# A 12-unit attention and rational-activation kernel: a new table of steps, and one PSUM slot for each chunk of the last unit

## Chip, cores and metric

The kernel runs on one core of a Trainium2 chip. The metric is device time in microseconds of one execution; 226.9 us is the median of three runs of the kernel before (226.29 to 226.97). The profile is of one further execution.

## What is computed

The reference, cut to what matters:

```python
# q, k, v, f_logit: (B, H, S, D) = (4, 8, 768, 48)
f = 1.0 / (1.0 + np.exp(-f_logit))
for t in range(S):
    state = f[:, :, t, :, None] * state + einsum('bhd,bhe->bhde', k[:, :, t], v[:, :, t])
    y[:, :, t] = einsum('bhd,bhde->bhe', q[:, :, t], state)
x = y.transpose(0, 2, 1, 3).reshape(3072, 384)
h = x @ w_in                                   # w_in (384, 2048)
P = a[0] + a[1] * h + a[2] * h**2 + a[3] * h**3
Q = 1.0 + abs(b[0]) * abs(h) + abs(b[1]) * h**2
out = (P / (Q + 1e-6)) @ w_out                 # w_out (2048, 384), out (3072, 384) f32
```

A gated linear attention with a recurrent state is followed by a two-layer feed-forward with a rational activation.

## The kernel before

The 4 batches times 768 tokens are cut into 12 units of 256 tokens (two chunks of 128). Unit n belongs to batch n mod 4; the state of a batch is handed from unit n to unit n + 4. Every unit passes through the same list of steps, each a small function of the kernel, and the program is one table, `ORDER`, of such steps. A step appends its instructions to its engines' queues in the order of the table, and semaphores between the engines follow from the data. The engines run their own queues in order, so the table sets two things: the order of steps on each engine, and which PSUM slot (`@0` to `@3`, two banks each, one tile at a time) a step takes. A step that takes a slot waits until the last reader of the slot's tile before it is done.

The steps by engine, with the unit as first argument and a range of blocks of 128 columns of d_ff (0 to 16) or of head pairs (0 to 4) as the last ones:

- SP's queue: `ld n f`, `ld n k`, `ld n q` (loads, L200), `ab_` (two small loads of coefficients for all partitions, L228 and L230), `so`, `s0` (stores, L584; `s1` issues on ACT's queue).
- POOL: `ld n v` (a load that casts to bf16), `wi` and `wo` (weights, L216 and L220), `vm` (copies of v, L388; `vm 0` on ACT), `zd` (L525) and `ta` (L559), which are DMAs that accumulate: z += h2 and gall += hy. `ca` and `cb` make the triangular and the identity matrix.
- ACT: `ef`, `ls` (log of the gate, L308, L313), `A` (exponentials of its running sum, L332), `ye` (L456), `ae` (L461), `hy` (PSUM to SBUF, L488), `sa` (square, L496), `ln` and `lz` (log of Q, L516 and L532), `ex` (1/Q by exp, L540), `oe` (result from PSUM to `osb`, L590).
- DVE: `xa` (scaled q and k, L337), `Te` (L356), `mk` (masked scores `scm`, L377), `st` (state, L465), `sq` (L492), `ab` (absolute value, L500), `p1`, `p2`, `pm`, `tv` (the polynomial, L545, L550, L555, L563), `gm` (times 1/Q, L568), `cz`, `cc`, `fa`, `fb` (constants), and `hv 0` (L210), a memset on `w_in_sb` behind which the `wi` loads wait.
- PE: `cs` (running sum, L323), `T` (transposes, L348), `sc` (scores, L369), `sv`, `id` (state, L413, L424, L428), `yb` (attention output, L394), `h` (x times w_in, L474), `u` (sums h2 and |h| in PSUM, L508), `o` (times w_out, L575; 12 units, two chunks j, 16 blocks m).

For half of the units' blocks Q is summed by PE (`u`, then `ln`), for the others by a DMA (`zd`, then `lz`); `ta` adds the two parts of the polynomial by a DMA, `tv` does it on DVE in the first unit and for half of the last. `hy` has three buffers, `h2` and `z` two, `gall` three, f, k, q and v three each, `osb` two.

In the last unit both chunks of the result lie in one tile, `op`, of slot 2. Chunk 1 is copied by DVE (`oe 11 1 2 v`), chunk 0 by ACT (`oe 11 0 1 s`):

```python
if sl is not None:
    s["op"] = slot(sl, [P, UB, 512], F32, "op")
for m in range(m0, m1):
    nc.tensor.matmul(s["op"][:, j, 0:DM], s["g"][:, m, C * j:C * j + C], w_out_sb[:, m, :],
                     start=(m == 0), stop=(m == KF - 1))
```

Of the kernel before, what the change touches and what calls it, by code (L numbers as in the profile page):

```python
# [19 lines left out]
b1_; cz 3; cb; ld 0 f 2 4; ld 0 f 0 2; ca; cz 0; ld 0 q 2 4; cz 2; ld 0 k 2 4; cz 1; cc; ef 0 2 4  # L20
ld 0 k 0 2; fa 0; ls 0 2 4; ld 0 q 0 2; ef 0 0 2; cs 0 2 4 @0; ls 0 0 2; ld 0 v; A 0 0 2 4
id 0 0 @1; A 0 1 2 4; xa 0 0 2 4; rg; cs 0 0 2 @2; ld 1 f; xa 0 1 2 4; ae 0; A 0 1 0 2; hv 0; ab_
T 0 2 4 @0; wi 0 4; A 0 0 0 2; xa 0 1 0 2; Te 0 2 4; xa 0 0 0 2; sc 0 1 @0; ld 1 k; T 0 0 2 @2
wi 4 8; mk 0 1; vc 0; Te 0 0 2; vm 0 0 s; sv 0; vm 0 1 s; ld 1 v; sc 0 0 @2; st 0 0; ld 1 q; wi 8 16
mk 0 0; id 0 1; st 0 1; yb 0 0 4 @2; ef 1; ld 2 f; fa 1; ls 1; ye 0; cs 1 @1; fb; h 0 0 4 @2; A 1 0
A 1 1; h 0 4 8 @1; hy 0 0 4; xa 1 1; ld 2 k; id 1 0 @2; hy 0 4 8; xa 1 0; ld 2 q; ae 1; sv 1; vm 1 0
vm 1 1; ab 0 0 8; T 1 @1; ld 2 v; sq 0 0 8; Te 1; u 0 0 4 @0; ef 2; ld 3 f; u 0 4 8 @3; st 1 0
# [603 lines left out]
```

## Time and profile before

| | |
|---|---|
| median of three runs | 226.9 us |
| profiled execution: its own time | 224.9 us |
| profiled execution: span of the program | 223.2 us |
| busy PE, DVE, ACT, POOL | 205.2, 203.3, 201.1, 70.4 us |
| TensorE clock granted | 1.00 of full speed |
| HBM read and written | 25.2 and 4.7 MB |

The profiled execution was 2.0 us shorter than the median of the runs. Its time is the span and 1.7 us around it. A row of the page gives line, engine, operation, tiles, shape and count, then busy time and mean duration, then idle time of the engine just before and what ended it. A line of the timeline gives start, length, engine, line, operation, and in brackets the idle time before it and the releaser.

### The profile page before, as it was taken

Reading aid. Unit: us, or ns where it says so; the run is one execution under the profiler, and the core shown is the slowest. Engines: PE = TensorE matmul, PEld = TensorE weight load, DVE = VectorE, ACT = ScalarE, POOL = GpSimd, SP = SyncE. Lnnn points to the kernel's source line nnn. Section 1 sums busy time; section 2 is a strip of 40 time slices with the busy share of each in tenths; the row PEclk is TensorE's granted clock in tenths of the full one; section 3 lists DMA queues with packets and bytes.
Section 4 is the critical chain, followed back from the end, with each engine's and each line's share of the span. In section 5 each row is a group of like instructions: output and inputs, shape, how many; then the busy total and the mean of one; then the engine's idle time right before and its main releaser. Section 6 shows DMA issues by size and latency. Waiting matters only on the chain.

```text
span 223.2 us, 7133 instructions
## 1 busy us (share of the span) xinstructions
PE 205.2 (92%) x3128; PEld 144.0 (65%) x3128; DVE 203.3 (91%) x248; ACT 201.1 (90%) x215; POOL 70.4 (32%) x94
## 2 busy tenths in 40 slices
PE   1786799999999997999999999999999999999991
PEld 1544378566766686567777668678578587785550
DVE  6865999999789997999999999999999999999960
ACT  5645599999999999999999999999999999999960
POOL 3662930021500333107334244041395311341000
PEclk9999999999999999999999999999999999999998
DMA  6999999998999999977999999938869999597434
GB/s 156 225 230 210 237 202 204 193 248 232 170 180 244 243 184 216 260 193 144 171 233 248 209 238 244 213 74 134 171 117 184 207 188 212 112 206 150 94 91 120
DMA packets 61984, 42.33 MB, mean 190 GB/s; under 512 B 51458, under 2 KB 57346, under 8 KB 61954
## 3 DMA queue, kind: packets, MB, share of 16 engines
q0 software_dynamic: 19648, 22.61, 61.6%
q1 hardware_dynamic: 42144, 19.08, 35.0%
q8 instruction: 24, 0.39, 0.6%
q10 hardware_dynamic: 162, 0.20, 0.2%
q14 instruction: 6, 0.05, 0.1%
HBM read 25.17 MB, written 4.72 MB: 134 GB/s over the span
## 4 chain that ended last, share of the span: by engine, by line
PE 62%; ACT 20%; DMA 7%; SPq 4%; issue 3%; DVE 3%
PE op L575 26%; PE hp L474 18%; DMA fn<-in_f_logit_dram 7%; PE u L508 5%; ACT hy L488 4%; PE y L394 4%; ACT lq L516 4%; ACT qi L540 3%; PE tp L348 3%; SPq L200 3%; ACT h L496 3%; ACT A L332 3%; PE sc L369 2%; ACT lsp L313 1%; ACT fn L308 1%
## 5 line engine op out<-in xcount | busy, mean ns | idle before, releaser
L474 PE MATMUL hp<-xT,w_in_sb 128*128 128x256 bf16 x576 | 68.6, 274 | 2.3 <-issue 1.3
L575 PE MATMUL op<-w_out_sb,gall 128*128 128x384 bf16 x384 | 68.7, 326 | 1.1 <-DVE osb L590 0.6
L474 PEld LDWEIGHTS <-w_in_sb 128*128 128x128 bf16 x576 | 55.9, 98 | 12.8 <-issue 3.6
L488 ACT CAST hy<-hp 128x1024 bf16<-128x1024 f32 x48 | 49.5, 1050 | 4.1 <-PE hp L474 4.0
L575 PEld LDWEIGHTS <-gall 128*128 128x128 bf16 x384 | 36.3, 98 | 25.0 <-issue 1.8
L540 ACT ACTIVATE qi<-lq 128x2048 bf16<-128x2048 f32 (+1 forms) x25 | 46.4, 1874 | 0.0
L559 POOL DMA_DIRECT2D gall<-hy x21 | 21.3, 1109 | 64.1 <-PE hp L474 16.4
L377 DVE TENSOR_TENSOR scm<-sc,mask 128x1024 bf16<-128x1024 f32 x24 | 28.7, 1217 | 3.3 <-PE sc L369 3.3
L568 DVE TENSOR_TENSOR gall<-gall,qi 128x2048 bf16<-128x2048 bf16 (+1 forms) x25 | 29.5, 1181 | 0.7 <-ACT qi L540 0.6
L555 DVE TENSOR_TENSOR gall<-gall,h 128x2048 bf16<-128x2048 bf16 (+1 forms) x25 | 29.3, 1177 | 0.0
L388 POOL COPY vmp<-vn 128x128 bf16<-128x128 bf16 x22 | 18.1, 927 | 22.9 <-DMA vn<-in_v_dram 22.9
L525 POOL DMA_DIRECT2D z<-h x12 | 13.2, 1097 | 37.9 <-ACT xT L456 13.4
L516 ACT ACTIVATE lq<-u 128x1024 f32<-128x1024 f32 x24 | 24.5, 1048 | 0.3 <-PE u L508 0.3
L532 ACT ACTIVATE lq<-z 128x2048 f32<-128x2048 bf16 x12 | 23.5, 1956 | 0.0
L492 DVE TENSOR_TENSOR h<-hy 128x2048 bf16<-128x2048 bf16 (+1 forms) x18 | 20.9, 1166 | 0.5 <-ACT hy L488 0.5
L332 ACT ACTIVATE A<-cs 128x768 f32<-128x768 f32 (+1 forms) x26 | 18.9, 786 | 0.7 <-PE cs L323 0.5
L500 DVE TENSOR_SCALAR z<-hy 128x2048 uint16<-128x2048 uint16 (+1 forms) x25 | 16.8, 676 | 1.5 <-ACT hy L488 1.5
L550 DVE TENSOR_SCALAR hy<-hy,a_sb 128x4096 bf16<-128x4096 bf16 (+2 forms) x15 | 16.9, 1128 | 0.1
L545 DVE TENSOR_SCALAR gall<-hy,a_sb 128x4096 bf16<-128x4096 bf16 (+2 forms) x15 | 16.9, 1126 | 0.0
L323 PE MATMUL cs<-lsp,Ui 128*128 128x384 bf16 (+1 forms) x39 | 11.1, 345 | 4.8 <-ACT lsp L313 4.6
L308 ACT ACTIVATE fn<-fn 128x768 f32<-128x768 f32 (+1 forms) x13 | 10.8, 830 | 4.8 <-DMA fn<-in_f_logit_dram 4.8
L356 DVE COPY qkT<-tp 128x2048 bf16<-128x2048 bf16 (+1 forms) x13 | 14.8, 1135 | 0.4 <-PE tp L348 0.4
(69 smaller groups left out, 272.9 us busy)
## 6 DMA issues: line engine op xcount, KB each, us to landing
gall<-hy POOLq DMA_DIRECT2D x21, 512.0 KB, 7.8
z<-h POOLq DMA_DIRECT2D x12, 512.0 KB, 7.3
fn<-in_f_logit_dram SPq DMA_DIRECT2D x11, 384.0 KB, 13.2
kn<-in_k_dram SPq DMA_DIRECT2D x11, 384.0 KB, 11.9
qn<-in_q_dram SPq DMA_DIRECT2D x11, 384.0 KB, 10.6
out_dram<-osb SPq DMA_DIRECT2D x22, 192.0 KB, 4.2
vn<-in_v_dram POOLq DMA_DIRECT2D x11, 192.0 KB, 8.8
w_out_sb<-in_moe_w_out_dram POOLq DMA_DIRECT2D x4, 384.0 KB, 11.6
```

Source lines behind the costliest of these rows:

```text
L332: nc.scalar.activation(t, src, AF.Exp, scale=1.0 if x else -1.0)
L377: nc.vector.tensor_mul(t, s["sc", g].rearrange("s r a i t -> s (r a) (i t)"), mb)
L474: nc.tensor.matmul(t[:, m - m0, :].rearrange("f (j t) -> f j t", j=UB), w_in_sb[:, kk, m * P:(m + 1) * P], s["x"][:, :, kk, :], start=(kk ...
L488: nc.scalar.copy(fl(big(s, "hy", "hy", 3), m0, m1), fl(s["hp", m0], 0, m1 - m0))
L492: nc.vector.tensor_mul(fl(big(s, "h2", "h2", 2), m0, m1), fl(s["hy"], m0, m1), fl(s["hy"], m0, m1))
L516: nc.scalar.activation(fl(s["lq", g], m0 - 8 * g, m1 - 8 * g), fl(s["u", m0], 0, m1 - m0), AF.Ln, scale=rsig2, bias=1.0 + 1e-6)
L532: nc.scalar.activation(fl(s["lq", g], m0 - 8 * g, m1 - 8 * g), fl(s["z"], m0, m1), AF.Ln, scale=rsig2, bias=1.0 + 1e-6)
L540: nc.scalar.activation(fl(s["qi", g], m0 - 8 * g, m1 - 8 * g), fl(s["lq", g], m0 - 8 * g, m1 - 8 * g), AF.Exp, scale=-1.0)
L555: nc.vector.tensor_mul(fl(s["g"], m0, m1), fl(s["g"], m0, m1), fl(s["h2"], m0, m1))
L559: nc.gpsimd.dma_start(out=fl(s["g"], m0, m1), in_=fl(s["hy"], m0, m1), accum_op=ALU.add)
L568: nc.vector.tensor_mul(fl(s["g"], m0, m1), fl(s["g"], m0, m1), fl(s["qi", g], m0 - 8 * g, m1 - 8 * g))
L575: nc.tensor.matmul(s["op"][:, j, 0:DM], s["g"][:, m, C * j:C * j + C], w_out_sb[:, m, :], start=(m == 0), stop=(m == KF - 1))
```

## The change

The table `ORDER` holds the same steps in another order, on every engine, and partly in other slots. Two steps go and four come: the copies of the last unit's chunks, `oe 11 1 2 v` and `oe 11 0 1 s`, are each replaced by two copies of half the columns, `oc 11 j 0 s` on ACT and `oc 11 j 1 v` on DVE. For the last unit `o` takes a slot for each chunk (`@1` and `@3`) in place of one for both. `wm`, a step that neither table calls, gets a wider tile. The steps on SP's and POOL's queues move too: `ld 1 q` ahead of `ld 1 k`, `ab_` behind both, `ld 4 f`, `ld 5 f` and `ld 6 f` further ahead among k and q, `ld 3 v` ahead of the `wo` loads, `ca` ahead of `cb`.

The beginning, some lines of the middle and the end of the table, and the code:

```diff
 ORDER = """
-b1_; cz 3; cb; ld 0 f 2 4; ld 0 f 0 2; ca; cz 0; ld 0 q 2 4; cz 2; ld 0 k 2 4; cz 1; cc; ef 0 2 4
-ld 0 k 0 2; fa 0; ls 0 2 4; ld 0 q 0 2; ef 0 0 2; cs 0 2 4 @0; ls 0 0 2; ld 0 v; A 0 0 2 4
-id 0 0 @1; A 0 1 2 4; xa 0 0 2 4; rg; cs 0 0 2 @2; ld 1 f; xa 0 1 2 4; ae 0; A 0 1 0 2; hv 0; ab_
-T 0 2 4 @0; wi 0 4; A 0 0 0 2; xa 0 1 0 2; Te 0 2 4; xa 0 0 0 2; sc 0 1 @0; ld 1 k; T 0 0 2 @2
-wi 4 8; mk 0 1; vc 0; Te 0 0 2; vm 0 0 s; sv 0; vm 0 1 s; ld 1 v; sc 0 0 @2; st 0 0; ld 1 q; wi 8 16
-mk 0 0; id 0 1; st 0 1; yb 0 0 4 @2; ef 1; ld 2 f; fa 1; ls 1; ye 0; cs 1 @1; fb; h 0 0 4 @2; A 1 0
-A 1 1; h 0 4 8 @1; hy 0 0 4; xa 1 1; ld 2 k; id 1 0 @2; hy 0 4 8; xa 1 0; ld 2 q; ae 1; sv 1; vm 1 0
-vm 1 1; ab 0 0 8; T 1 @1; ld 2 v; sq 0 0 8; Te 1; u 0 0 4 @0; ef 2; ld 3 f; u 0 4 8 @3; st 1 0
-ln 0 0 4; p1 0 0 8; id 1 1; sc 1 0 @1; ln 0 4 8; st 1 1; sc 1 1 @0; mk 1 0; ls 2; ex 0 0 8; mk 1 1
-id 2 0 @3; ld 3 k; cs 2 @1; pm 0 0 8; yb 1 0 4 @0; A 2 1; wo 8 12; h 0 12 16 @2; p2 0 0 8; ye 1
+cz 2; ca; ld 0 f 2 4; cz 0; ld 0 f 0 2; ld 0 q 2 4; cb; cc; cz 1; ld 0 k 2 4; cz 3; ld 0 k 0 2
+ef 0 2 4; ld 0 q 0 2; ls 0 2 4; ef 0 0 2; cs 0 2 4 @0; ld 0 v; b1_; ls 0 0 2; ld 1 f; A 0 0 2 4
+cs 0 0 2 @1; A 0 1 2 4; id 0 0 @2; A 0 1 0 2; hv 0; xa 0 1 2 4; wi 0 4; xa 0 0 2 4; ae 0; A 0 0 0 2
+ld 1 q; T 0 2 4 @0; ld 1 k; xa 0 0 0 2; xa 0 1 0 2; fa 0; T 0 0 2 @1; vc 0; ab_; wi 4 8; sv 0
+Te 0 2 4; rg; st 0 0; vm 0 0 s; ld 1 v; Te 0 0 2; ef 1; ld 2 f; id 0 1; sc 0 1 @0; st 0 1; wi 8 16
+sc 0 0 @1; ls 1; mk 0 0; vm 0 1 s; id 1 0 @2; cs 1 @3; mk 0 1; A 1 1; yb 0 0 4 @0; ye 0; A 1 0
+h 0 0 4 @0; fa 1; xa 1 0; ld 2 k; h 0 4 8 @3; hy 0 0 4; ld 2 q; xa 1 1; ae 1; fb; hy 0 4 8; T 1 @0
+sq 0 0 8; sv 1; vm 1 1; vm 1 0; ab 0 0 8; ef 2; ld 3 f; ld 2 v; p1 0 0 8; u 0 0 4 @3; ls 2; ld 3 v
+Te 1; u 0 4 8 @1; ln 0 0 4; wo 4 8; st 1 0; sc 1 0 @0; wo 0 4; ln 0 4 8; cs 2 @3; mk 1 0; sc 1 1 @1
+A 2 1; mk 1 1; h 0 12 16 @0; ex 0 0 8; pm 0 0 8; yb 1 0 4 @1; ld 3 k; xa 2 1; id 1 1; ye 1; p2 0 0 8
...
-o 0 1 4 8; ex 1 0 8; h 2 0 4 @2; pm 1 0 8; ld 5 f; gm 0 8 16; h 2 4 8 @0; hy 2 0 4; xa 3 1; ef 4
-o 0 1 8 12; sq 1 8 16; ld 5 k; o 0 1 12 16; sa 2 4 8; ld 4 v; sv 3; sa 2 0 4; p2 1 0 16; o 0 0 8 12
-vm 3 0; ls 4; vm 3 1; ld 5 q; u 1 12 16 @2; st 3 0; ta 1 0 8; hy 2 4 8; pm 1 8 16; o 0 0 12 16
-ln 1 12 16; id 3 1; ld 6 f; T 3 @0; st 3 1; ta 1 8 16; ef 5; ab 2 0 8; u 1 8 12 @3; Te 3; oe 0 0 2 s
-zd 2 0 8; h 2 12 16 @2; ln 1 8 12; so 0 0 2; ls 5; sc 3 1 @3; sc 3 0 @0; h 2 8 12 @1; mk 3 1; ld 6 k
-ex 1 8 16; ld 5 v; mk 3 0; cs 4 @3; vm 4 1; hy 2 8 12; vm 4 0; cs 5 @0; A 4 0; yb 3 0 4 @1; gm 1 0 8
-A 4 1; ye 3; xa 4 0; o 1 0 0 4 @3; hy 2 12 16; o 1 1 0 4; xa 4 1; ld 6 q; h 3 4 8 @1; A 5 0
+o 0 0 0 4 @2; ex 0 8 16; st 3 0; yb 2 0 4 @3; tv 0 8 16; id 3 1; ld 5 v; o 0 1 0 4; st 3 1; ye 2
+o 0 0 4 8; gm 0 8 16; vm 3 1; ln 1 4 8; h 2 4 8 @3; p1 1 0 16; ls 4; ex 1 0 8; o 0 1 4 8; xa 3 0
+h 2 0 4 @0; ld 6 f; ab 1 8 16; ld 4 q; hy 2 4 8; pm 1 0 8; o 0 1 8 12; o 0 0 8 12; sa 2 0 4
+sq 1 8 16; T 3 @1; ef 5; o 0 1 12 16; p2 1 0 16; hy 2 0 4; ld 5 k; o 0 0 12 16; sa 2 4 8
+u 1 8 12 @0; Te 3; ta 1 0 8; oe 0 0 2 s; u 1 12 16 @3; ab 2 0 8; ln 1 8 12; sc 3 0 @2; sc 3 1 @1
+ln 1 12 16; mk 3 0; h 2 8 12 @0; ls 5; mk 3 1; cs 4 @2; hy 2 8 12; ld 6 k; cs 5 @3; pm 1 8 16
+ld 5 q; A 4 0; yb 3 0 4 @0; ld 7 f; A 4 1; xa 4 0; h 2 12 16 @1; ta 1 8 16; ye 3; xa 4 1; vm 4 1
+A 5 0; vm 4 0; h 3 0 4 @0; gm 1 0 8; hy 2 12 16; vm 5 1; zd 2 0 8; A 5 1; T 4 @2; p1 2 0 16; ld 6 v
...
-st 4 1; pm 2 0 8; ld 8 f; sv 5 @2; oe 1 0 2 s; id 5 0; ef 7; sq 3 0 8; T 5 @3; ta 2 0 8; so 1 0 2
-sv 6 @3; ln 3 8 12; gm 2 0 8; id 6 0; cs 7 @1; ld 9 f; ae 6; ln 3 12 16; st 6 0; sc 5 1 @2; pm 3 0 8
+p2 2 0 16; ln 2 8 12; o 1 0 8 12; xa 5 1; hy 3 12 16; ta 2 0 8; o 1 1 8 12; ld 8 f; pm 2 8 16
+h 3 8 12 @1; A 6 0; st 5 0; so 1 0 2; zd 3 0 8; gm 2 0 8; ef 7; id 5 1; h 4 8 12 @3; ld 7 v; A 6 1
...
-ta 4 8 16; o 3 1 0 4; gm 3 8 16; ae 7; ef 9; yb 6 0 4 @0; lz 4 0 8; st 7 0; o 3 0 4 8; p1 5 0 16
-gm 4 8 16; o 3 1 12 16; sa 6 0 4; o 4 0 0 4 @3; Te 7; hy 6 0 4; o 4 1 0 4; ld 11 f; ef 10; sq 6 8 16
+pm 4 8 16; o 3 1 0 4; ae 7; ye 6; o 3 0 4 8; st 7 0; ta 4 8 16; p1 5 0 16; ex 4 0 8; o 3 1 4 8
+hy 6 8 12; gm 4 8 16; T 7 @3; A 8 0; o 4 0 0 4 @2; ab 5 8 16; hy 6 4 8; o 4 0 4 8; Te 7; sa 6 4 8
...
-ln 11 12 16; o 10 1 12 16; pm 11 8 12; o 11 0 0 4 @2; p2 11 8 12; ex 11 8 12; tv 11 8 12; o 11 1 0 4
-ex 11 12 16; o 11 0 4 8; gm 11 8 12; o 11 1 4 8; oe 10 0 2 s; gm 11 12 16; o 11 1 8 12; so 10 0 2
-o 11 1 12 16; o 11 0 8 12; oe 11 1 2 v; o 11 0 12 16; s1 11 1 2; s0 11 1 2; oe 11 0 1 s; s1 11 0 1
+o 11 0 0 4 @1; ex 11 8 12; tv 11 8 12; o 11 1 0 4 @3; tv 11 12 16; ex 11 12 16; o 11 0 4 8
+gm 11 8 12; o 11 1 4 8; oe 10 0 2 s; gm 11 12 16; o 11 1 8 12; so 10 0 2; o 11 1 12 16; o 11 0 8 12
+oc 11 1 0 s; oc 11 1 1 v; o 11 0 12 16; s1 11 1 2; s0 11 1 2; oc 11 0 0 s; oc 11 0 1 v; s1 11 0 1
 s0 11 0 1
 """
...
     def o(n, j, m0, m1, sl=None):
         s = unit(n)
-        if sl is not None:
-            s["op"] = slot(sl, [P, UB, 512], F32, "op")
+        if sl is not None and n == B * NCC - 1:
+            s["op", j] = slot(sl, [P, 512], F32, "op")
+        elif sl is not None:
+            t = slot(sl, [P, UB, 512], F32, "op")
+            s["op"] = t
+            for i in range(UB):
+                s["op", i] = t[:, i]
         for m in range(m0, m1):
-            nc.tensor.matmul(s["op"][:, j, 0:DM], s["g"][:, m, C * j:C * j + C], w_out_sb[:, m, :],
+            nc.tensor.matmul(s["op", j][:, 0:DM], s["g"][:, m, C * j:C * j + C], w_out_sb[:, m, :],
                              start=(m == 0), stop=(m == KF - 1))
...
+    def oc(n, j, c, eng):
+        s = unit(n)
+        if "osb" not in s:
+            s["osb"] = ms.tile([P, UB, DM], F32, name="osb")
+        cc = slice(c * DM // 2, (c + 1) * DM // 2)
+        (nc.scalar.copy if eng == "s" else nc.vector.tensor_copy)(s["osb"][:, j, cc], s["op", j][:, cc])
```

## The prediction

> **What bounds the kernel now.** I read the page's busy shares, then its chain, then the waits of each engine, then the timeline at the places that the waits name. The shares and the chain:
>
> ```profile
> PE 205.2 (92%) x3128; PEld 144.0 (65%) x3128; DVE 203.3 (91%) x248; ACT 201.1 (90%) x215; POOL 70.4 (32%) x94
> PE 62%; ACT 20%; DMA 7%; SPq 4%; issue 3%; DVE 3%
> ```
>
> Three engines are within 2% of each other, so none is the bound alone. The chain has three stages: loads until 24.8 us, ACT until 63.8, PE to the end. The joints show in the timeline (start, length, engine, operation, idle before it and who ended it):
>
> ```profile
> 24.80 0.84 ACT L308 ACTIVATE fn<-fn 128x768 f32<-128x768 f32 x1 [3.42 <-DMA fn<-in_f_logit_dram]
> 26.61 0.42 PE L369 MATMUL sc<-qkT 48*64 48x128 bf16 x16 [0.91 <-ACT lq L516]
> ...
> 59.38 2.36 DVE L377 TENSOR_TENSOR scm<-sc,mask 128x1024 bf16<-128x1024 f32 x2 [1.20 <-PE sc L369]
> 63.05 0.96 DVE L337 TENSOR_TENSOR qkp<-qn,A 128x768 bf16<-128x768 f32 x1 [0.17 <-ACT A L332]
> 65.37 0.69 DVE L500 TENSOR_SCALAR z<-hy 128x2048 uint16<-128x2048 uint16 x1 [0.49 <-ACT hy L488]
> ...
> 85.56 1.38 PE L474 MATMUL hp<-xT,w_in_sb 128*128 128x256 bf16 x11 [1.14 <-issue]
> ...
> 217.67 0.56 DVE L590 COPY osb<-op 128x384 f32<-128x384 f32 x1 [1.81 <-PE op L575]
> 218.28 0.81 PE L575 MATMUL op<-w_out_sb,gall 128*128 128x384 bf16 x4 [0.65 <-DVE osb L590]
> 219.13 0.48 ACT L590 COPY osb<-op 128x384 f32<-128x384 f32 x1 [3.31 <-PE op L575]
> ```
>
> Line 1 is step `ef 2`: ACT stood idle 3.4 us for unit 2's f_logit. The next four are handovers between engines in a bad order. The 1.14 us of "issue" is no step's fault. The last three are the tail: PE has its last 4 matmuls left and waits 0.65 us for a DVE copy.
>
> **PE's account.** Successive rows overlap slightly, so I count from start to start: `h` 1.31 us, four matmuls of `o` 0.65, `u` 0.86, `yb` 1.12 (0.97 for units 0 to 3), `T` 0.89, `cs` 0.66, `sc` 0.33, `sv` 0.37, `id` 0.38 or 0.16. From `cs 2` at 28.47 there stand 46 `h`, 96 quarters of `o`, 22 `u`, 11 `yb`, 10 each of `T`, `cs` and `sv`, 20 `sc`, 15 `id`: 183.6 us. PE ends at 219.09, so it loses 219.09 - 28.47 - 183.6 = 7.0 us: 0.8 in the tail (the wait and its drain), 1.3 to "issue", 4.9 waiting for ACT and DVE in many small pieces.
>
> [...] Between 29 and 38 us the two queues moved nearly equal counts of packets of very unequal size:
>
> ```profile
> q0 software_dynamic: 1638, 1.20, 85.7%
> q1 hardware_dynamic: 1615, 0.61, 38.8%
> ```
>
> [...] the 0.65 us come from both being one tile. [...]
>
> **The change, part by part.**
>
> *Tail.* With a slot for each chunk, PE no longer waits for the copy of chunk 1: -0.65 us, and nothing is late next, since `o 11 0 12 16` reads `gall` made long before. The last copy falls from 128x384 (0.48) to halves on ACT and DVE. The 128x768 copy takes 0.84, so 384 columns cost 0.36 and half a copy 0.48 - 0.18 = 0.30: -0.18. Two instructions are added (one ACT, one DVE, 0.3 each), both where those engines are idle. The two stores of each chunk now wait for both copies. The edit of `wm` issues nothing: neither table calls it. Sum -0.8; bounds -0.5 and -1.0.
>
> *Reordering, 29 to 210 us.* No other step is added or removed. What an order costs can be read without a clock: follow a loop of steps over the engines and add the work along it. Before, `h 2 0 4` (PE) feeds `hy 2 0 4` (ACT); from there to the end of `hy 2 12 16` ACT has 14.7 us of work (with `ef 4`, `ls 4`, `ef 5`, `ex 1 8 16` between); that feeds `ab 2 8 16` on DVE, which stands 6.9 us of work behind `st 3 1`; and `st 3 1` frees the slot of `u 1 8 12`, which stands 6.2 us behind `h 2 0 4` on PE. 14.7 - 6.9 - 6.2 = 1.6, with three handovers of 0.1 about 1.9 us that somebody must idle. The three DVE waits of 1.20, 0.17 and 0.49 above are just that: 1.86. In the new order the four ACT steps leave this stretch, so ACT's leg is 9.6, and `st 3 1` stands eight places earlier on DVE: the loop is slack. I took the worst such loop in each stretch of about 30 us. Before: 0.25, 1.9, 0.7, 0.8, 0.4, 0.85, together 4.9, which is what the account found. After: 1.1, 0.05, 0.25, 0.15, 0.3, 0.9, together 2.7. So -2.2 us; bounds 0 (other waits come in their place) and -3.5.
>
> *Accumulating DMAs (POOL's queue).* The new order leaves less room between a `ta` and the `gm` that reads it. For `gm 4 8 16` DVE has 6.5 us of other work after `pm 4 8 16` (16 before), for `gm 2 0 8` 6.7 (11 before), 1 0 8 6.9, 5 0 8 7.7. The page's median from issue to landing is 7.8 us and the issue lags some 0.5:
>
> ```profile
> gall<-hy POOLq DMA_DIRECT2D x21, 512.0 KB, 7.8
> ```
>
> but `ta 1 0 8` took 4.7 when its queue was empty. At 4.7 there is no wait; at 8.3 the four cost 1.8 + 1.6 + 1.4 + 0.6 = 5.4 us on DVE, and PE soon waits with it. I take +0.8; bounds 0 and +5.4.
>
> *Prologue.* `hv 0`, the memset that holds the w_in loads back, moves before the first `xa` (some 4.5 us instead of 6.97), so POOL's `wi` packets start 2 to 3 us earlier and share the DMA engines with unit 0's v (landing 9.37). `sv 0` now stands ahead of `sc 0 1` and `sc 0 0` on PE and waits for v, so `yb 0` comes 2 to 3 us later than 13.0. Cover: ACT has 3.4 us to spare before `ef 2`. `ab_` (1.9 us of SP issue) moves behind `ld 1 q` and `ld 1 k`, which refills SP's queue sooner; `ld 2 f` keeps its place there with the same packets ahead. Its landing stays near 24.8, give or take 1.5 for the altered mixing. Then `ls 2` at once, `cs 2` at 27.3 instead of 28.5, but `sc 1 1` waits for `ln 0 4 8` until 28.2 (26.6 before), so `h 1 4 8` starts near 31.7 against 31.51. Net +0.5; bounds -1 and +2.5. [...] `o 0 0 0 4` needs w_out only at 45. Later SP loads (`ld 5 f`, `ld 6 f` ahead of q and k) keep 27 us or more from a free buffer to the first use, against landings of 11 to 13: nothing, covered by ACT's and PE's own work; late SP stores wait behind loads with nobody waiting but the buffer `osb`.
>
> Sum: -0.8 - 2.2 + 0.8 + 0.5 = -1.7 on the profiled execution, 223.2 us of span to 221.5, its own time 224.9 to 223.2. The median of the runs shown is 226.9, 2.0 above that execution, so 225.2.
>
> **Rivals.**
> 1. *The new order works as above:* 225.2, from 223 to 226.2. For it: the loop at 58 to 66 us is in the trace to a tenth. Chance 0.50.
> 2. *The gain is eaten:* waits removed return as small ones, or `ld 2 f` lands 1.5 later, which delays ACT and through its slots PE, one for one. -0.8 - 2.2 + 0.8 + 2.0 is close to 0: about 226.8. Chance 0.13.
> 3. *Slower by the accumulating DMAs:* with landings at 8 us or more, `gm` waits on DVE at four to six places; `o`, `mk` and `st` queue behind it, and PE and ACT with them. -0.8 - 2.2 + 5.4 + 0.5 = +2.9: 229.8; half of that price, 227 to 228. It decides from about 2.5 us of such waits on. For it: 7.8 is a median, and the room is under it at four places; before, only `gm 1 0 8`, `gm 2 8 16` and three near the end had so little. Against it: unstacked transfers land in 4.5 to 5.1. With a late `ld 2 f` on top it gives the upper end. Chance 0.37.
> 4. *The slot change does nothing* (the copies still serialise): 0.8 us less gain, inside the cases above.
>
> **The numbers.** A measurement of this kernel can tell about 0.3% (0.7 us) from no change. Faster 0.50, within 0.13, slower 0.37. The range for 8 in 10 runs from 222.4 (the loops at -3.5, a prologue at -0.5) to 229.6 (rival 3 whole); the likeliest case's own range is 223 to 226.2.
>
> **What would show it.** Right: no PE wait for `osb`, two copies of 128x192 on each engine, DVE's waits for `scm` and ACT's for `hy` under half of what the waits between 28.5 and 216 us list before (2.8 and 2.1 us). Wrong: DVE waits of over 0.5 us at L568's counterpart ended by a DMA (rival 3); `ef 2` after 26 us (rival 2); PE waiting on ACT evenly all along would mean that ACT, not the order, sets the pace.

## The result, and the profile after

The changed kernel takes **233.7 us** (median of four runs, 232.69 to 234.65) where the kernel before took 226.6 beside it: a ratio of **1.031**, with an interval of 1.026 to 1.037. That is slower, by 7 us, and beyond the upper end of the predicted range. The profiled execution took 234.3 us, with a span of 232.6.

The page of the kernel after begins with the busy time of each engine; further down stand the shares of the chain that ended last, by engine and by line:

```profile
PE 209.2 (90%) x3113; PEld 146.0 (63%) x3128; DVE 205.4 (88%) x249; ACT 202.2 (87%) x216; POOL 71.6 (31%) x94
DVE 26%; DMA 23%; issue 15%; PE 15%; ACT 13%; SPq 4%; POOL 1%; ACTq 0%; DVEq 0%; POOLq 0%
DMA gall<-hy 12%; DMA b<-in_moe_b_dram 6%; PE op L582 5%; DMA z<-h 5%; DVE gall L556 4%; SPq L201 4%; DVE scm L378 4%; PE hp L475 4%; DVE gall L569 3%; DVE h L493 3%; DVE qkp L338 3%; ACT qi L541 3%; PE u L509 3%; DVE gall L546 2%; DVE z L501 2%
```

Busy time hardly moved; the idle time is what grew. Before, PE held 62% of the chain and DMA 7%. Now PE holds 15% and DMA 23%, and the DMAs at the head of the second list are the two kinds of accumulating transfer (`gall<-hy` is `ta`, `z<-h` is `zd`) and a load of 1 KB, `b`. So transfers now stand on the chain that ended last. Which of them cost time is a question for the experiments.

The account of the prediction (starts of PE's steps, less their work) places the loss. "Loss" is time from one start to the other minus the work of the steps between:

| | before | after | difference |
|---|---|---|---|
| start of `h 1 4 8` | 31.5 | 38.3 | +6.8 |
| loss from `h 1 4 8` to `h 5 0 4` | 4.7 | 3.4 | -1.3 |
| loss from `h 5 0 4` to `h 9 0 4` | 0.7 | 4.7 | +4.1 |
| loss from `h 9 0 4` to `o 11 0 12 16` | 1.4 | 0.6 | -0.8 |

With 0.4 us of work that has moved across the first mark this is the 9.1 us by which PE's last four matmuls start later (227.4 against 218.3); the copies behind them add 0.3. The medians differ by less, 7 us, because the profiled execution of the kernel before was 1.7 us under its median. The first row varies most between executions: the new start came to `h 1 4 8` at 37.0 in a joined kernel below, and the old start at 33.3 in the kernel with the new tail alone. In two of four stretches the change gained what was forecast in kind; the start and the third stretch lost far more.

**The start.** Lines of the timeline of DVE (start, length, engine, line, operation, and in brackets the idle time before it and who ended it):

```profile
24.28 0.17 DVE L278 TENSOR_SCALAR bm<-b 128x2 uint32<-128x2 uint32 x1 [8.68 <-DMA b<-in_moe_b_dram]
25.44 0.96 DVE L338 TENSOR_TENSOR qkp<-qn,A 128x768 bf16<-128x768 f32 x1
26.31 0.95 DVE L338 TENSOR_TENSOR qkp<-kn,A 128x768 bf16<-128x768 f32 x1
```

The first line is `fa 1`, waiting 8.7 us for `ab_`'s load, which was issued at 10.47 and took 13.8 us (4.5 before). Behind it in DVE's queue stand `xa 1 0` and `xa 1 1`. Before, they stood at 19.35 and 17.49, and `xa 1 0` waited for q:

```profile
17.49 0.96 DVE L337 TENSOR_TENSOR qkp<-kn,A 128x768 bf16<-128x768 f32 x1 [2.14 <-ACT A L332]
19.35 0.96 DVE L337 TENSOR_TENSOR qkp<-qn,A 128x768 bf16<-128x768 f32 x1 [0.90 <-DMA qn<-in_q_dram]
```

The wait for `b` looks like the whole cause of the late start. The experiments show that it isn't.

**The middle.** The waits between 40 and 229 us (engine, line, for whom: total, times, longest), then the place of the longest in the timeline:

```profile
ACT lq L533 <- DMA z<-h: 2.7, 2, 2.3
DVE gall L569 <- DMA gall<-hy: 2.3, 5, 0.9
DVE scm L378 <- PE sc L370: 0.6, 3, 0.2
ACT hy L489 <- PE hp L475: 0.4, 2, 0.2
```

```profile
119.23 1.91 ACT L533 ACTIVATE lq<-z 128x2048 f32<-128x2048 bf16 x1 [2.26 <-DMA z<-h]
121.24 0.56 DVE L466 TENSOR_TENSOR state<-sv,alast 128x384 bf16<-128x384 f32 x1 [1.78 <-ACT alast L462]
121.85 0.32 PE L425 MATMUL sv<-state,ident 128*128 128x384 bf16 x1 [1.48 <-DVE state L466]
161.94 1.23 DVE L569 TENSOR_TENSOR gall<-gall,qi 128x2048 bf16<-128x2048 bf16 x1 [0.89 <-DMA gall<-hy]
```

The last two of the waits are those of the loops, 2.8 and 2.1 us before: the new order did remove them. The first two did not exist before. The timeline shows how one wait travels: `lz 4 0 8` stands idle on ACT for `zd 4 0 8` (11.2 us from issue to landing; 7.8 before), so `ae 7` behind it is late, so `st 7 0` on DVE, so `id 7 1` on PE.

**The tail:**

```profile
226.94 0.32 ACT L605 COPY osb<-op 128x192 f32<-128x192 f32 x1 [1.14 <-PE op L582]
227.29 0.36 DVE L605 COPY osb<-op 128x192 f32<-128x192 f32 x1 [1.46 <-ACT osb L605]
228.27 0.32 ACT L605 COPY osb<-op 128x192 f32<-128x192 f32 x1 [1.01 <-PE op L582]
228.62 0.36 DVE L605 COPY osb<-op 128x192 f32<-128x192 f32 x1 [0.97 <-ACT osb L605]
```

PE waits for no copy any more. But DVE's half waits for ACT's half: the two run one after the other, 0.7 us where one copy of the whole chunk took 0.48.

### The profile page after: what moved, and what is told of

It reads as the page before. It is cut to its first block, busy times and chain, and to the rows that moved or that the text cites. A ratio compares the mean times of both kernels' runs of the same rounds, so it can differ in the third digit from the quotient of the medians.

```text
span 232.6 us, 7113 instructions
## 1 busy us (share of the span) xinstructions
PE 209.2 (90%) x3113; PEld 146.0 (63%) x3128; DVE 205.4 (88%) x249; ACT 202.2 (87%) x216; POOL 71.6 (31%) x94
## 4 chain that ended last, share of the span: by engine, by line
DVE 26%; DMA 23%; issue 15%; PE 15%; ACT 13%; SPq 4%; POOL 1%; ACTq 0%; DVEq 0%; POOLq 0%
DMA gall<-hy 12%; DMA b<-in_moe_b_dram 6%; PE op L582 5%; DMA z<-h 5%; DVE gall L556 4%; SPq L201 4%; DVE scm L378 4%; PE hp L475 4%; DVE gall L569 3%; DVE h L493 3%; DVE qkp L338 3%; ACT qi L541 3%; PE u L509 3%; DVE gall L546 2%; DVE z L501 2%
## 5 line engine op out<-in xcount | busy, mean ns | idle before, releaser
L475 PE MATMUL hp<-xT,w_in_sb 128*128 128x256 bf16 x576 | 70.8, 279 | 2.8 <-DMA w_in_sb<-in_moe_w_in_dram 0.9
L475 PEld LDWEIGHTS <-w_in_sb 128*128 128x128 bf16 x576 | 56.9, 100 | 14.7 <-issue 3.7
L489 ACT CAST hy<-hp 128x1024 bf16<-128x1024 f32 x48 | 48.5, 1037 | 4.1 <-PE hp L475 4.0
L560 POOL DMA_DIRECT2D gall<-hy x21 | 20.4, 974 | 81.1 <-DVE gall L556 18.6
L389 POOL COPY vmp<-vn 128x128 bf16<-128x128 bf16 x22 | 19.3, 903 | 10.6 <-DMA vn<-in_v_dram 5.9
L526 POOL DMA_DIRECT2D z<-h x12 | 14.9, 1239 | 24.6 <-DVE h L493 8.5
L333 ACT ACTIVATE A<-cs 128x768 f32<-128x768 f32 (+1 forms) x26 | 19.5, 780 | 2.6 <-PE cs L324 2.5
L201 POOL DMA_DIRECT2D vn<-in_v_dram x11 | 12.6, 1147 | 24.2 <-issue 23.5
L551 DVE TENSOR_SCALAR hy<-hy,a_sb 128x4096 bf16<-128x4096 bf16 (+2 forms) x15 | 17.2, 1146 | 0.1
L349 PE MATMUL tp<-ident,qkp 128*128 128x128 bf16 x192 | 13.7, 227 | 3.5 <-ACT fn L309 2.1
L509 PEld LDWEIGHTS <-ident 128*128 128x128 bf16 x96 | 9.3, 100 | 11.4 <-issue 3.0
## 6 DMA issues: line engine op xcount, KB each, us to landing
kn<-in_k_dram SPq DMA_DIRECT2D x11, 384.0 KB, 10.4
w_out_sb<-in_moe_w_out_dram POOLq DMA_DIRECT2D x4, 384.0 KB, 11.1
```

Source lines behind the costliest of these rows:

```text
L201: eng.dma_start(out=s[what][:, hh].rearrange("p h i d -> p h (i d)"), in_=src[s["b"], hh, t0:t0 + NT, :].rearrange("h (p i) d -> p h (i d) ...
L475: nc.tensor.matmul(t[:, m - m0, :].rearrange("f (j t) -> f j t", j=UB), w_in_sb[:, kk, m * P:(m + 1) * P], s["x"][:, :, kk, :], start=(kk ...
L489: nc.scalar.copy(fl(big(s, "hy", "hy", 3), m0, m1), fl(s["hp", m0], 0, m1 - m0))
```

## Experiments on the start

The first theory was that the late `b` makes the late start. Two runs move `ab_` alone, in both directions, and one moves the waiting instruction.

`ab_` early in the changed kernel:

```diff
-ld 1 f; ...; ld 1 q; T 0 2 4 @0; ld 1 k; ...; vc 0; ab_; wi 4 8
+ld 1 f; ab_; ...; ld 1 q; T 0 2 4 @0; ld 1 k; ...; vc 0; wi 4 8
```

> The changed kernel, with one step moved back: `ab_` (the loads of moe_b and moe_a to 128 partitions) stands right behind `ld 1 f` on SP's queue, ahead of `ld 1 q` and `ld 1 k`, as before the change. Theory (the late b: `fa 1` waits 8.7 us for it on DVE, with `xa 1 0`, `xa 1 1` and so all of unit 1 behind it): b lands by about 12 us, `fa 1` doesn't wait, `hy 1 4 8` starts near 34 instead of 39.8, and the time falls by 4 to 6 us, to 228 to 229.5. Rival (the accumulating transfers and the lower clock of PE at 25 to 35 us set the time, the late start is absorbed by the slack of the loops behind it): it falls by less than 1.5 us.

Measured: 1.030 of before (1.021 to 1.038), median 232.3. Nobody waits for `b` any more, `h 1 4 8` starts at 35.9 in place of 38.3, and the time cannot be told from the changed kernel's 1.031. The number is the rival's, though the start as a whole does count, as the joined orders show below.

`ab_` late in the kernel before:

```diff
-hv 0; ab_; T 0 2 4 @0; ...; st 0 0; ld 1 q; wi 8 16
+hv 0; T 0 2 4 @0; ...; st 0 0; ld 1 q; ab_; wi 8 16
```

> The kernel before, with only `ab_` moved: behind `ld 1 k` and `ld 1 q` on SP's queue. Theory (the late b): b lands some 10 us later than the 10.8 us of before, `fa 1` waits for it on DVE ahead of `xa 1 1`, and the time rises by 4 to 6 us, to 230.5 to 233. Rival (the late start is absorbed): less than 1.5 us more than before.

Measured: 0.998 (0.995 to 1.001). The theory's 4 to 6 us do not come, although `fa 1` waits 5.4 us for `b`:

```profile
18.93 0.17 DVE L274 TENSOR_SCALAR bm<-b 128x2 uint32<-128x2 uint32 x1 [5.42 <-DMA b<-in_moe_b_dram]
```

Most of that wait is covered: before, `xa 1 0` waited for q until 19.35, and PE waited for v of unit 1 and came to `T 1` at 22.2; now `T 1` starts at 22.8. But the edit does a second thing. SP's queue is freer without `ab_`'s 1.9 us of issuing in the middle of it, and `ef 2` starts at 22.5 rather than 24.8. The run shows the sum of the two and not that the wait is free: `u 0 0 4` starts at 24.7 here, at 23.3 before.

`fa 1` and `fb` late in the changed kernel, with `b` left late:

```diff
-h 0 0 4 @0; fa 1; xa 1 0; ...; ae 1; fb; hy 0 4 8; ...; p1 0 0 8
+h 0 0 4 @0; xa 1 0; ...; ae 1; hy 0 4 8; ...; fa 1; fb; p1 0 0 8
```

> The changed kernel with the load `ab_` left where it is, late, and `fa 1` and `fb` moved on DVE to just ahead of `p1 0 0 8`, their first user, behind `xa 1 0`, `xa 1 1`, `Te 1`. Theory (the cost is DVE's order behind the waiting instruction, not the transfer): most of the gain of moving the load, 3.5 to 6 us faster than the changed kernel, 227.5 to 230. Rival (k and q of unit 1 land late as well, k at 23.3 us, so `xa 1 1` waits anyway): `xa 1 1` starts after 23.3 whatever DVE does, and the gain is under 2 us.

Measured: 1.037 (1.030 to 1.044), no gain. In the trace `h 1 4 8` starts at 36.1 in place of 38.3, but PE's loss from `h 5 0 4` to `h 9 0 4` is 7.7 us in place of 4.7, part of it at a lower clock (0.67 from 150 to 155 us; last section). The rival's reason is in DVE's timeline, where the wait for `b` has given way to one for k of unit 1 (the `xa 1 1` of this line began at 26.31 in the changed kernel):

```profile
24.40 0.96 DVE L334 TENSOR_TENSOR qkp<-kn,A 128x768 bf16<-128x768 f32 x1 [1.82 <-DMA kn<-in_k_dram]
```

So unit 1's own loads are late too. What moved them? `hv 0` releases the w_in loads on POOL's queue at 4.6 us in place of 7.4. Put back, on top of an early `ab_`:

```diff
-A 0 1 0 2; hv 0; xa 0 1 2 4; wi 0 4; xa 0 0 2 4; ae 0
+A 0 1 0 2; xa 0 1 2 4; xa 0 0 2 4; hv 0; wi 0 4; ae 0
```

> The changed kernel with `ab_` early (as in the experiment on it) and `hv 0` and `wi 0 4` moved back behind `xa 0 0 2 4`, so that the w_in loads on POOL's queue start near 7 us instead of 4.6. Theory (the early w_in packets share the DMA engines with unit 1's f, q and k on SP's queue, and k of unit 1, landing at 23 us instead of 14.6, then holds `xa 1 1`): k of unit 1 lands 2 to 4 us earlier, `h 1 4 8` starts near 33 instead of 35.9, and the time is 2 to 3.5 us under that of `ab_` early alone (232.3), 229 to 230.3. Rival (the order q ahead of k, or PE's `sv 0` ahead of `sc 0 1`, makes it late, not w_in): under 1 us.

Measured: 1.012 (1.006 to 1.019), median 229.8, as the theory said; `h 1 4 8` starts at 32.7. And the same move alone, the other way, in the kernel before:

```diff
-xa 0 0 2 4; ...; A 0 1 0 2; hv 0; ab_; T 0 2 4 @0; wi 0 4
+hv 0; wi 0 4; xa 0 0 2 4; ...; A 0 1 0 2; ab_; T 0 2 4 @0
```

> The kernel before with only `hv 0` and `wi 0 4` moved ahead, in front of `xa 0 0 2 4`, so that the w_in loads on POOL's queue start near 4.6 us instead of 7.4. Theory (they take the DMA engines from SP's loads of unit 1): f, k and q of unit 1 land 2 to 4 us later, `h 1 4 8` starts 2 to 3 later than 31.5, the time rises by 1.5 to 3, to 228 to 229.5. Rival (the early w_in helps `h 0 0 4` as much as it hurts, and only together with q ahead of k and `sv 0` ahead of `sc` is it late): within 1 us of before.

Measured: **1.012** (1.009 to 1.015), median 229.3: one memset that moves two places on DVE costs 2.7 us. Its timeline shows the three loads that pay, k, q of unit 1 and f of unit 2:

```profile
19.12 0.96 DVE L334 TENSOR_TENSOR qkp<-kn,A 128x768 bf16<-128x768 f32 x1 [3.36 <-DMA kn<-in_k_dram]
24.91 0.96 DVE L334 TENSOR_TENSOR qkp<-qn,A 128x768 bf16<-128x768 f32 x1 [4.83 <-DMA qn<-in_q_dram]
27.11 0.84 ACT L305 ACTIVATE fn<-fn 128x768 f32<-128x768 f32 x1 [5.62 <-DMA fn<-in_f_logit_dram]
```

How they come to be late is in the DMA view from 4 to 16 us (queue, packets, MB, time of its packets as a share of the 16 engines). First the kernel before, then this one; q1 is SP's queue, q0 POOL's:

```profile
q1 hardware_dynamic: 6005, 2.16, 71.8%
q0 software_dynamic: 687, 0.61, 33.0%
```

```profile
q1 hardware_dynamic: 5174, 1.84, 64.6%
q0 software_dynamic: 1111, 0.83, 47.5%
```

POOL's queue moves 0.22 MB more and SP's 0.32 MB less, and at this point SP's queue carries what the engines wait for.

## Experiments on the two halves of the order

To price start and body apart, the two tables were joined at `hy 1 4 8`, where the sets of steps already issued differ by only 12 of some 120 steps.

```diff
+(kernel before: all steps up to hy 1 4 8)
+(changed kernel: all other steps, in its order)
-T 2 @1; ... h 1 12 16 @2; ... cs 3 @3; ... u 0 12 16 @3
+T 2 @2; ... h 1 12 16 @0; ... cs 3 @2; ... u 0 12 16 @0
```

> Two orders joined. The steps up to `hy 1 4 8` (about 34 to 40 us into the run) stand as in the kernel before, all later steps as in the changed kernel, tail included; four slot numbers at the joint differ. From starts of PE's steps, the changed kernel is 6.8 us later than the one before at `h 1 4 8` and loses 8.7 us from there to its last four matmuls, where the one before loses 6.7. Theory (both parts count, and add): this kernel takes the time of before plus about 2, 228 to 229.5. Rival 1 (the start is absorbed, the body is all): as slow as the changed kernel, 232 or more. Rival 2 (the start is all): the time of before, 226 to 227.

The reverse, with the steps up to `hy 1 4 8` from the changed kernel and all others from the one before:

> The other way round: the steps up to `hy 1 4 8` as in the changed kernel, all later ones as in the kernel before, its tail included; 16 slot numbers behind the joint differ. Theory (both parts count, and add): the time of before plus 4 to 6.5, 230.5 to 233. Rival 1 (the start is absorbed): under 1.5 above before. Rival 2 (the start is all): plus 7, 233 to 234.

Measured: old start with new body 1.016 (1.009 to 1.023); new start with old body 1.025 (1.019 to 1.032). Both parts cost, neither rival holds; the first, at 231.0 us, lies above the 228 to 229.5 that were expected. The loss from `h 5 0 4` to `h 9 0 4` goes with the body and not with the start: 5.5 us in the first, 0.65 in the second. The two ratios add up to 1.041, more than the 1.031 of the whole, though their intervals just allow it.

## Experiments on the body

`lz 4 0 8` behind other work of ACT (`ab_` early as above):

```diff
-yb 6 0 4 @0; lz 4 0 8; id 7 0; ...; ae 7; ye 6; o 3 0 4 8
+yb 6 0 4 @0; id 7 0; ...; ae 7; ye 6; lz 4 0 8; o 3 0 4 8
```

> The changed kernel with `ab_` early and one step moved on ACT: `lz 4 0 8`, which waited 2.0 us there for the accumulating transfer `zd 4 0 8` (10.9 us from issue to landing), stands behind `ae 7` and `ye 6` instead of ahead of them. Theory (that wait holds `ae 7`, so `st 7 0` on DVE and `id 7 1` on PE, which waited 1.2 us): ACT's wait for z goes, the loss of PE between `h 5 0 4` and `h 7 0 4` falls from 3.3 to about 1.5 us, and the time by 1.5 to 2, to 230.3 to 230.8. Rival (the next transfers, for `gm 4 8 16` and `gm 5 0 8`, are late by themselves and take the wait over): PE's loss from `h 5 0 4` to `h 9 0 4` stays near 5.5 and the time moves by under 0.7.

Measured: 1.019 (1.012 to 1.027), median 231.4. ACT's wait falls from 2.0 to 0.8 us, but DVE waits 0.6, 0.85, 1.3 and 1.8 for the next four transfers, and PE's loss stays at 5.3 us from `h 5` to `h 9`. The time is 0.85 us under that of `ab_` early alone, between the theory and the rival, and not to be told from it. More room at three places at once, on the joined order (old start, new body):

```diff
-ab 2 0 8; ... vm 5 1; zd 2 0 8;          vm 7 0; ...; zd 4 0 8
+ab 2 0 8; zd 2 0 8; ... vm 5 1;          zd 4 0 8; vm 7 0
-lz 4 0 8; id 7 0; ...; ae 7; ye 6; ...; ef 9          gm 5 0 8; cs 9 @3; ...; pm 6 0 8; ...; xa 9 1
+id 7 0; ...; ae 7; ye 6; ef 9; lz 4 0 8               cs 9 @3; ...; pm 6 0 8; ...; xa 9 1; ...; gm 5 0 8
```

> The joined order (start of before, body and tail of the changed kernel; 230.96) with more room between the accumulating transfers and their readers at the three places on its path: on POOL's queue `zd 2 0 8` moved ahead, right behind `ab 2 0 8`, and `vm 7 0` behind `zd 4 0 8`; on ACT `ef 9`, `ae 7` and `ye 6` ahead of `lz 4 0 8`; on DVE `pm 6 0 8` and `xa 9 1` ahead of `gm 5 0 8`. Theory (too little room behind the transfers is what the body loses): the waits of ACT for z and of DVE for gall fall from 4.9 us to under 1.5, PE's loss between `h 5 0 4` and `h 9 0 4` from 5.5 to 2 or 3, and the time by 2 to 3, to 228 to 229. Rival (the two queues together carry too much at 100 to 155 us, the transfers land late wherever they are placed): the loss stays over 4.5 and the time within 1 of 230.96.

Measured: 1.021 (1.013 to 1.028), median 231.1, no gain, as the rival said. The waits at `lz 4 0 8` and `gm 5 0 8` are gone and others stand in their place; the waits for these transfers add up to 4.4 us from 40 to 229 us, against 4.6 in the joined order:

```profile
75.56 1.23 DVE L565 TENSOR_TENSOR gall<-gall,qi 128x2048 bf16<-128x2048 bf16 x1 [1.55 <-DMA gall<-hy]
125.26 1.23 DVE L565 TENSOR_TENSOR gall<-gall,qi 128x2048 bf16<-128x2048 bf16 x1 [1.27 <-DMA gall<-hy]
159.03 1.23 DVE L565 TENSOR_TENSOR gall<-gall,qi 128x2048 bf16<-128x2048 bf16 x1 [0.84 <-DMA gall<-hy]
```

The first is the doing of the edit: `zd 2 0 8`, moved ahead on POOL's queue, makes `ta 1 8 16` land after 10.4 us instead of 6. The last transfer took 14.6 us. So moving single transfers and readers only moves the lateness, and the next experiment takes the other queue's packets away from the transfers:

```diff
-ld 9 k; ld 10 k; ld 11 k; so 2 0 2; so 3 0 2; so 4 0 2
...
-s["qk"[x]][:, hh]
+s["q" if n > 8 else "qk"[x]][:, hh]
```

> The joined order (start of before, body and tail of the changed kernel; 230.96) with less traffic on SP's queue between 92 and 155 us: the k of units 9, 10 and 11 isn't loaded (their `xa n 1` reads q instead) and the rows of units 2, 3 and 4 aren't stored, so this part of the computation is left out. That takes some 2.3 of the 5.9 MB off SP's queue there; no step of PE, ACT, DVE or POOL goes. Theory (the accumulating transfers land late [...]): `zd 4 0 8`, `ta 4 0 8`, `zd 6 0 8`, which took 11.1 to 11.3 us, land in 8 to 9.5, the waits of ACT and DVE for them fall from 4.3 us in all to under 2, PE's loss between `h 5 0 4` and `h 9 0 4` from 5.5 to 2 to 3.5, and the time to 228 to 229.5. Rival (POOL's own transfers queue up behind each other and need no one else to be late): over 10 us each, loss over 4.5, time within 1 of 230.96.

Measured: **1.006** (1.003 to 1.009), where the joined order had 1.016 (1.009 to 1.023). That is some 2.3 us by the ratios and 3.9 by the medians (227.0 and 231.0). PE's loss from `h 5 0 4` to `h 9 0 4` falls from 5.5 to **1.2** us. Time and loss both end below what the theory, that SP's loads and stores make the transfers late, expected. The DMA view from 92 to 155 us, first of the joined order, then of this kernel:

```profile
q0 software_dynamic: 5684, 6.40, 62.1%
q1 hardware_dynamic: 13328, 5.91, 39.6%
```

```profile
q0 software_dynamic: 5881, 7.08, 69.6%
q1 hardware_dynamic: 9208, 3.49, 23.3%
```

With 2.4 MB less on SP's queue, `zd 4 0 8`, `ta 4 0 8` and `zd 6 0 8` land after 9.2, 8.6 and 7.8 us (11.1, 11.3 and 11.2). The waits from 40 to 229 us, again joined order first:

```profile
DVE gall L565 <- DMA gall<-hy: 2.4, 2, 1.9
ACT lq L529 <- DMA z<-h: 2.2, 1, 2.2
```

```profile
DVE gall L564 <- DMA gall<-hy: 0.6, 2, 0.4
ACT lq L528 <- DMA z<-h: 0.4, 1, 0.4
```

Between 92 and 180 us no compute engine of the joined order waited for one of the loads or stores that are left out here, so what went is not their own lateness. The control makes the same edit in the kernel before.

> Control to the experiment with less traffic: the kernel before with the same work left out (k of units 9, 10 and 11 not loaded, their `xa n 1` reads q; the rows of units 2, 3 and 4 not stored). Theory (only the new order has the accumulating transfers on its path; the old one has 10 to 20 us of room behind them): PE's loss between `h 5 0 4` and `h 9 0 4` goes from 0.65 to 0.3 to 0.65 and the time stays within 0.7 of before. Rival (less traffic helps any order): 2 or more under before.

Measured: 1.001 (0.998 to 1.004), with the loss at 0.65 as before. Less traffic does nothing for this order, which has the room. Lateness by itself does not cost either: four of the 33 accumulating transfers of the kernel before took 10.2 to 10.7 us, and nobody waited for them. The body's loss needs both, transfers slowed by SP's loads and stores (11.1 us for `zd 4 0 8`, 9.2 with 2.4 MB of them left out) and an order that reads them sooner (9.0 us from its issue to the point where ACT is free for it in the changed kernel, 20.7 before).

## The tail alone, and a version that is faster than both

The tail of the change in the kernel before (`o 11 0` in @2, `o 11 1` in @1, and `oc` for `oe`):

```diff
-oe 11 1 2 v; o 11 0 12 16; s1 11 1 2; s0 11 1 2; oe 11 0 1 s; s1 11 0 1; s0 11 0 1
+oc 11 1 0 s; oc 11 1 1 v; o 11 0 12 16; s1 11 1 2; s0 11 1 2; oc 11 0 0 s; oc 11 0 1 v; s1 11 0 1; s0 11 0 1
```

> The kernel before with only the tail of the change: the last unit's two chunks of `o` each in a slot of its own (@2 and @1), and each copied as two halves by ACT and DVE (`oc`). Theory of the prediction: -0.8 us. Theory from the trace of the changed kernel (the halves of one chunk run one after the other, 0.32 + 0.36, in place of one copy of 0.48): PE's wait of 0.65 goes, the last copy gets 0.2 longer, so -0.3 to -0.5. Rival (copy and stores set the end, PE's wait doesn't count): 0 to +0.3.

Measured: 1.001 (0.997 to 1.005), not to be told from no change. In the trace PE's loss from `h 11 0 4` to `o 11 0 12 16` goes from 0.83 to 0.01 us, and from there to the end of the span it takes 5.23 us in place of 4.95: -0.8 and +0.3. The interval holds both the trace's theory and the rival.

The pieces that did no harm point to a version: the order of before, `ab_` late, `fa 1` where nobody stands behind it, and a slot for each chunk with the copies whole.

```diff
-hv 0; ab_; ...; ld 1 q; ...; ld 2 f; fa 1; ...; cs 1 @1; fb; ...; xa 1 0
+hv 0; ...; ld 1 q; ab_; ...; ld 2 f; ...; cs 1 @1; ...; xa 1 0; fa 1; fb
-o 11 1 0 4
+o 11 1 0 4 @1
```

> A version meant to beat both: the kernel before with `ab_` behind `ld 1 q` on SP's queue, `fa 1` and `fb` moved on DVE behind `xa 1 0`, and the last unit's two chunks in a slot each, copied whole (chunk 1 by DVE, chunk 0 by ACT). Theory (SP's queue is free sooner, so `ef 2` starts near 22.5 as with `ab_` late instead of 24.8, and nobody waits for b; PE doesn't wait for the copy of chunk 1): 1.5 us less at the start, 0.5 to 0.8 at the end, so about 1 per cent under before, 224 to 225 where before is at 226.5. Rival (`xa 1 0` waits for q of unit 1 in any case and sets the start): only the tail's 0.5 to 0.8, not to be told from no change.

Measured: **0.986** (0.980 to 0.991), median 223.8 (222.7 to 224.6): faster than both kernels. `ef 2` starts at 21.3, `h 1 4 8` at 30.8, nobody waits for `b`, and the end is clean:

```profile
216.59 0.56 DVE L594 COPY osb<-op 128x384 f32<-128x384 f32 x1 [1.16 <-PE op L578]
217.89 0.48 ACT L594 COPY osb<-op 128x384 f32<-128x384 f32 x1 [2.50 <-PE op L578]
```

From the start of the last four matmuls to the end of the span it takes 4.97 us, so the whole copies keep the 0.8 that the halves partly gave back. The rest can be read beside the run with `ab_` late alone (0.998). The two kernels differ only in the tail and in the place of `fa 1` and `fb`, and this one is 1.2% faster, some 2.7 us; in the traces it is 0.8 us ahead in the tail and 1.4 at `h 1 4 8`. So moving `fa 1` and `fb` brings part of the gain. The 5.4 us of waiting for `b` were not free there, and the earlier `ef 2` hid what they cost.

Last, the new order's slack loops without its start and without its late body:

```diff
+(the faster version: all steps up to hy 1 4 8)
+(changed kernel: its steps up to xa 5 0)
+(the faster version: all other steps)
```

> Three pieces: the start of the version that beat both kernels (223.8), the changed kernel's order from `hy 1 4 8` to its `xa 5 0` (about 34 to 83 us), then the order of before with the tail of that version; five slot numbers differ. Theory (the prediction's term for the loops is right where no transfer masks it: from `h 1 4 8` to `h 5 0 4` PE lost 4.7 us before and 2.7 to 3.4 in the changed order): 1 to 2 us less, 222 to 223. Rival (behind this start the new stretch loses as much, as it did in the joined order, 4.25): within 0.7 of 223.8. Joined badly (a transfer or slot late at the second joint, near 83 us): 225 or more.

Measured: 1.000 (0.997 to 1.003), median 226.7, so worse than the faster version; of the expected outcomes it is the number of the bad joint. Why is not shown, since there is no trace of a typical execution of this kernel. One candidate stands in the traces of other kernels: from its issue to the point where ACT is free for `lz 2 0 8`, `zd 2 0 8` has 7.9 us in the changed kernel and 13.0 in the one before. It took 8.3 us in the changed kernel, and ACT waited 0.5 us for it; with `hv 0` put back ACT waited 1.7.

## Why the prediction was wrong, step by step

**The prologue's term failed first: +0.5 forecast, bounds -1 and +2.5; the new start costs 2.5% (1.9 to 3.2%), some 5.7 us.** Three of its steps are at fault. (1) "`hv 0` ... so POOL's `wi` packets start 2 to 3 us earlier and share the DMA engines with unit 0's v": the start was right, the sharer was wrong. v landed at 9.5 (9.4 before); f and k of unit 1, behind it on SP's queue, paid, with 13.2 and 23.3 us (10.6 and 14.6 before). q, now ahead of k, landed at 17.2 (19.3). By itself, in the kernel before, this move costs 2.7 us. (2) `ab_` was costed as 1.9 us of SP's issuing and its landing was not asked for; the waiting instruction `fa 1` has `xa 1 0` and `xa 1 1` behind it on DVE. Putting it back moves `h 1 4 8` by 2.4 us in the trace, but no run shows it in the time by itself: with k late as well, it gave nothing that can be measured. (3) "Cover: ACT has 3.4 us to spare before `ef 2`" named the wrong cover. `ef 2` came at 25.6, within the limit that was set, while the path to `h 1 4 8` ran over unit 1's `xa`, `T 1` and the slots of `u 0 0 4` and `u 0 4 8`. With both moves undone `h 1 4 8` starts at 32.7, inside the 31.5 to 33.3 of the old start, and the time (1.012) is not above that of the old start with the new body (1.016). So `hv 0` and `ab_` together hold the cost of the start, and nothing is seen of the rest (q ahead of k, `sv 0` ahead of `sc`). How the two share it is open: `hv 0` put back with `ab_` left late was not tried.

**The accumulating DMAs: +0.8 forecast, +4.1 in the trace; the mechanism was rival 3's, the term was under-sized.** The bound of +5.4 held it, but three things were off. The list held only `gm`; the longest wait, 2.3 us, is at an `lz`, whose `zd 4 0 8` has 9.0 us from issue to the point where ACT is free for it, where it had 20.7. Landing was taken between 4.7 and 8.3 us; `zd 4 0 8`, `ta 4 0 8` and `ta 6 0 8` took 11.2, 11.6 and 12.5. The trace of the kernel before had landings of 10.2 to 10.7 already, so 8.3 was no upper bound; the median even fell with the change, from 7.8 to 7.2 for `ta`. The sign that the prediction named for this rival came: DVE waits of up to 0.9 us at `gm`, ended by a DMA. And the central value leaned on unstacked transfers, while the new order issues them in bunches: `ta 3 0 8`, `zd 4 0 8` and `ld 8 v` within 1.1 us. The prediction counted POOL's loads against SP's, but it went both ways here: with the w_in loads early in the kernel before, SP's queue moved 1.84 MB in place of 2.16 between 4 and 16 us, and with 2.4 MB less on SP's queue `zd 4 0 8` landed after 9.2 us in place of 11.1. The nearly equal packet counts that the prediction read between 29 and 38 us are those of one stretch: between 4 and 16 us SP's queue moved 6005 packets and POOL's 687. How the two queues share the DMA engines is not shown.

**The loops: -2.2 forecast, -1.3 in the trace** from `h 1 4 8` to `h 5 0 4`, where most of it was promised. The mechanism is right: DVE's waits for `scm` fell from 2.8 to 0.6 us, ACT's for `hy` from 2.1 to 0.4, under half as the prediction asked. But in no run did it shorten the time, since the same reordering takes room from the transfers.

**The tail: -0.8 forecast, about -0.5 in the trace of the tail alone.** PE's wait went as forecast. The term for the last copy was wrong in sign, -0.18 against +0.3: two halves cost 0.32 and 0.36 one after the other. Rival 4 was half right: the slots do their work, the copies still serialise. The prediction asked what holds chunk 0's matmuls behind chunk 1's copy, but not what could hold one half behind the other. The two halves lie in one tile of `op` and in one of `osb`; what orders them was not separated.

The chance for slower, 0.37, was too small, and the upper end of 229.6 took one large loss but not two; it even lies under the 229.8 that the prediction itself summed for rival 3. The rivals were each one mechanism; the start and the transfers came together, and in both what one queue moved slowed the other: SP's loads beside the early w_in loads (waits of 3.4 us for k and 4.8 for q of unit 1 in the kernel before with `hv 0` early), the accumulating transfers beside SP's loads and stores (11.1 us against 9.2). What stays open is why the two halves add up to somewhat more than the whole. A start 3.2 us earlier (`hv 0` and `ab_` back, against `ab_` alone) was still 2.4 us ahead at `h 5 0 4` and only 0.7 by `h 8 0 4`; but between the two that execution had 3.4 us at half the clock, so it does not show that the body takes an earlier start back.

## What to carry to other kernels

When an order is changed, follow every transfer and not only every engine: for each, from issue to first reader, and what else is on the DMA engines then, because an order that is slack between engines can be tight behind its transfers (here 9.0 us of room for one that took 11.2). A load that is released earlier can take its bandwidth from what is queued beside it, here 0.32 MB of SP's between 4 and 16 us, so ask who is waited for next. A wait seen in a trace, even the longest one with a queue behind it, is a cause only if taking it away moves the end: here 5.4 us of waiting left the time of one order unchanged, mostly covered and the rest made up for by the same edit, and 8.7 us of it hid a second late load in another.

## What the hardware did that was not expected

TensorE's granted clock fell to 0.50, in three executions behind 3.41 us in which PE was busy for 0, 1.18 and 1.77 us. The rows are cut where the clock changes and 3.41 us ahead of its fall, as long as one low stretch below lasted (us, then busy time and instructions of PE, PEld, DVE, ACT, POOL, the granted clock, DMA share, GB/s). First the changed kernel, then the kernel before with `hv 0` early:

```profile
24.47:27.88 3.41, 1.18 (x19) 0.91 (x19) 3.19 (x12) 2.59 (x3) 0.00 (x0) 1.00 1.68 186
27.88:34.71 6.83, 6.01 (x69) 2.57 (x72) 5.41 (x7) 2.08 (x3) 1.25 (x1) 0.50 1.25 223
```

```profile
22.15:25.56 3.41, 0.00 (x0) 0.00 (x0) 0.65 (x1) 0.00 (x0) 3.20 (x5) 1.00 1.38 241
25.56:28.98 3.42, 3.05 (x20) 2.21 (x21) 3.17 (x4) 0.84 (x1) 0.40 (x2) 0.50 1.30 200
```

In the second kernel no matmul ran for 3.41 us, then the clock fell. In the first it fell although PE had been busy for 1.18 of the 3.41 us. Busy time alone does not decide it: with `fa 1` late PE was busy for 1.58 us from 27.02 to 30.43 and the clock stayed at 1.00; with `hv 0` put back it was busy for 1.77 us from 144.62 to 148.03 and the clock fell. What decides it is not shown.

What it costs shows where PE has no other wait. In that last run the clock stood at 0.50 from 148.03 to 151.44 while PE was busy throughout. PE's loss from `h 5 0 4` to `h 9 0 4` was 7.3 us there and 5.5 with `ab_` early alone, where the order is the same and the mean clock was 1.00: 1.8 us more. In the changed kernel the low clock came before `h 1 4 8`, which the joined kernel with the same start, at a mean clock of 0.999, reached 1.3 us sooner. Its runs fit that, 234.3 and 234.7 us at a mean clock of 0.985 and 232.7 and 233.1 at 0.999 and 1.000, but four runs do not show a price in time: with `fa 1` late a run at 0.988 took 232.7 us and one at 0.997 took 234.1.

A load of 1 KB (`b`) took 4.5 us in the kernel before, ahead of two loads of 384 KB on SP's queue, and 9.9 and 7.2 us behind them (`ab_` late alone, and the faster version), each time with the w_in loads released late on POOL's queue. With those released early it took 9.6 us ahead (`ab_` early in the changed kernel) and 13.8 behind. Its landing followed its place and its company, not its size.
